# Weight sums of the seven products: from GpSimd to VectorE, with a new order of all steps

## Chip, cores, metric

One Trainium2 chip; the kernel runs on one core. The metric is the device time of one execution in microseconds (us), as the median of several runs, lower is better. PE is TensorE (PEld its weight loads), DVE is VectorE, ACT is ScalarE, POOL is GpSimd, SP is SyncE, which issues most DMAs.

## What is computed

A retention layer with a decaying state is followed by a mixture layer. Batch 4, 8 heads of 64, sequence 768; the second layer is 512 wide with 1024 hidden units. Cut to what matters:

```python
for b in range(nb):                     # blocks of 64 positions
    intra = einsum(einsum(qb, kb) * Dmask, vb)
    out[:, :, sl] = intra + einsum(qb * lam_pow, kv_state)
    kv_state = lam ** 64 * kv_state + einsum(kb * rev_pow, vb)
x = out in (batch, position, 512)
xk = mu_k * x + (1 - mu_k) * x_prev     # x_prev: one position earlier
xr = mu_r * x + (1 - mu_r) * x_prev
k = maximum(xk @ w_k, 0)
v = k * k @ w_v
return sigmoid(xr @ w_r) * v
```

## The kernel before

The 768 positions are six tiles (n = 0 to 5) of 128 positions for all four batches; the 512 channels are four pairs of heads (hp). Products of the second layer are made in float32 quality from two float32r parts of each operand, a high and a low one (`PASSES`, line 423): three matmuls in place of one. ACT makes the high part by a cast (x_high, k_high, piece_high), DVE the low part by a subtraction (x_low, k_low, piece_low).

Tiles 0 and 1 go through the second layer tile by tile. Tiles 2 and 3, and then 4 and 5, go as a pair by a scheme of seven products in place of eight (`strassen`, step M): the weight matrix is cut in quarters 11, 12, 21, 22, and four sums of quarters ("1" to "4") stand beside the quarters as stationary operands; sums of the moving quarters (T1 to T4, sum_moving, step Ts) stand on the other side. KSEQ and VSEQ (line 573) list the seven products of the w_k and of the w_v layer with their operands.

The sums of weights are made once, in the middle of the kernel:

- For w_k: nine additions or subtractions over "lines" of 128 x 1024 (add_lines, step Wp, line 558), in two scratch tiles at home kf0 and kf1, then for each of the four sums a cast to the high part on ACT (sum_high, Wq) and a subtraction for the low part (sum_low, Wr, line 566), in the homes wk0 to wk3, and a store to DRAM (store_sum, Wt). M.0,k,2 to M.0,k,5 read them from SBUF: M.0,k,2 needs Wr of "2", M.0,k,3 that of "1", M.0,k,4 that of "4", M.0,k,5 that of "3".
- For w_v: the quarters are stored to DRAM (keep_set, Ws) and come back in four chunks (load_chunk, Wl, two DMAs of 512 KB each, line 519) into the homes big1, big2, big3 and big1 again (`ROOM`, line 765), which hold the squared hidden units of tile 1 until its V product has read them. For each chunk the high and low parts are joined (join_chunk, Wa, 128 x 1024), four sums of quarters are made (sum_chunk, Wc, 128 x 256 each, one after the other), ACT casts the high part (chunk_high, Wh), the low part is a subtraction (chunk_low, Wd), and two stores go to DRAM (store_chunk, Wo).

Wa, Wc, Wd, Wp and Wr, 37 instructions in all, are issued on POOL. POOL's other work is small: for each mix, copies of 128 x 4 elements that shift the row of positions by one (mix_begin, step i; mix_edge, step z). mix (step f) on DVE waits for them and for ACT's scaled copy (mix_prev, e).

The order of all work is written out by hand as a list of 1222 steps, `ORDER` (line 769). A step is a letter for a function and its arguments; the table is at line 737. Every instruction is kept in program order on its engine (`InOrder`, line 25), SP's DMAs among them, so an engine that waits at a step holds up all its later steps. In the list: A scores, a decay, q decay_queries, U sums, u odd_state, n next_state, B values (0 the first part, 1 the part with the state) for tile and pair; Y a piece of tile 1's V product (six matmuls), o v_out; X a column of the gate product of a late tile, Xo its sigmoid; M.pair,layer,product,column,half six matmuls of a product; j what follows a k product; Th and Td the parts of a moving operand; v, vg, vO the end of a v product, its gate and its store.

```python
    def join_chunk(c):
        t = chunks[c]
        gpsimd.tensor_tensor(t[:, 0], t[:, 0], t[:, 1], op=ALU.add)
```

The functions in full, with the profile's line numbers:

Of the kernel before, what the change touches and what calls it, by code (L numbers as in the profile page):

```python
# [904 lines left out]
```

## Time and profile before

| | us |
|---|---|
| median of 3 runs | 407.19 (406.86 to 409.12) |
| the profiled execution | 404.04 |
| its span, first to last instruction | 402.3 |
| PE busy | 377.5 (94%) |
| DVE busy | 271.7 (68%) |
| ACT busy | 243.5 (61%) |
| POOL busy | 111.2 (28%) |
| mean granted TensorE clock | 0.989 of full |

The profile is of one execution. Busy time is the time in which an engine has an instruction under way, including time in which that instruction is held up after it began. Matmul ends are modelled, so a busy PE is not a PE at its peak. "Idle before, releaser" is what ended an engine's wait.

### The profile page before, as it was taken

Reading aid. Unit: us, or ns where it says so; the run is one execution under the profiler, and the core shown is the slowest. Engines: PE = TensorE matmul, PEld = TensorE weight load, DVE = VectorE, ACT = ScalarE, POOL = GpSimd, SP = SyncE. Lnnn points to the kernel's source line nnn. Section 1 sums busy time; section 2 is a strip of 40 time slices with the busy share of each in tenths; the row PEclk is TensorE's granted clock in tenths of the full one; section 3 lists DMA queues with packets and bytes.
Section 4 is the critical chain, followed back from the end, with each engine's and each line's share of the span. In section 5 each row is a group of like instructions: output and inputs, shape, how many; then the busy total and the mean of one; then the engine's idle time right before and its main releaser. Section 6 shows DMA issues by size and latency. Waiting matters only on the chain.

```text
span 402.3 us, 9529 instructions
## 1 busy us (share of the span) xinstructions
PE 377.5 (94%) x4052; PEld 305.4 (76%) x4052; DVE 271.7 (68%) x349; ACT 243.5 (61%) x385; POOL 111.2 (28%) x191
## 2 busy tenths in 40 slices
...
GB/s 297 408 343 338 350 15 327 163 113 348 318 396 3 105 347 295 339 255 310 184 111 210 287 255 270 220 328 158 58 329 117 104 210 235 124 139 132 194 145 156
DMA packets 29994, 90.89 MB, mean 226 GB/s; under 512 B 2432, under 2 KB 14848, under 8 KB 26240
## 3 DMA queue, kind: packets, MB, share of 16 engines
...
q14 instruction: 10, 0.08, 0.1%
...
## 4 chain that ended last, share of the span: by engine, by line
PE 65%; DVE 12%; ACT 8%; DMA 5%; POOL 5%; issue 2%; SPq 1%; ACTq 0%; POOLq 0%; DVEq 0%
PE dense_m L33 58%; DMA chunk<-sets_v 4%; PE xp_sc L33 4%; POOL chunk L33 3%; DVE t L33 2%; ACT top L33 2%; PE sc_sc L33 2%; DVE qv L33 2%; ACT kf L33 2%; DMA in<-parts 2%; PE u_u L33 1%; DVE xq L33 1%; POOL ts L33 1%; SPq L33 1%; DVE raw L33 1%
## 5 line engine op out<-in xcount | busy, mean ns | idle before, releaser
L33 PE MATMUL dense_m<-t,ws 128*128 128x512 f32 x528 | 122.5, 391 | 0.6 <-DVE snap L33 0.6
L33 PEld LDWEIGHTS dense_m<-t,ws 128*128 128x128 f32 x528 | 98.4, 188 | 21.9 <-DVE snap L33 1.1
L33 PE MATMUL dense_m<-xr,wr 128*128 128x512 f32 x192 | 45.6, 393 | 1.8 <-DVE xr L33 1.8
L33 PE MATMUL dense_m<-xk,wk 128*128 128x512 f32 x192 | 46.7, 397 | 0.0
L33 PE MATMUL dense_m<-wv,k 128*128 128x512 f32 x192 | 45.6, 394 | 0.0
L33 PEld LDWEIGHTS dense_m<-xr,wr 128*128 128x128 f32 x192 | 35.6, 188 | 10.0 <-DVE xr L33 2.6
L33 PEld LDWEIGHTS dense_m<-xk,wk 128*128 128x128 f32 x192 | 35.4, 188 | 8.6 <-issue 0.7
L33 PEld LDWEIGHTS dense_m<-wv,k 128*128 128x128 f32 x192 | 35.5, 188 | 7.8 <-DVE wv L33 0.2
L33 POOL COPY ts<-lastw 128x4 f32<-128x4 f32 x48 | 15.2, 331 | 87.5 <-DVE xr L33 76.2
L33 ACT ACTIVATE c<-c 128x1024 f32<-128x1024 f32 x28 | 29.0, 1058 | 13.9 <-DVE c L33 13.8
L33 ACT ACTIVATE ts<-xp_sc,omu 128x512 f32<-128x512 f32 x40 | 25.9, 688 | 18.9 <-PE xp_sc L33 13.1
L33 POOL TENSOR_TENSOR chunk<-chunk 128x256 f32<-128x256 f32 (+2 forms) x24 | 32.9, 1372 | 7.5 <-DMA chunk<-sets_v 7.0
L33 POOL COPY ts<-ts 128x4 f32<-128x4 f32 x48 | 13.7, 291 | 71.5 <-ACT ts L33 71.4
L33 DVE TENSOR_TENSOR t<-c,t 128x1024 fp32r<-128x1024 f32 x20 | 24.2, 1221 | 10.0 <-ACT t L33 10.0
L33 DVE SCALAR_TENSOR_TENSOR ts<-xp_sc,smalls,ts 128x512 f32<-128x512 f32 x24 | 17.3, 746 | 19.8 <-POOL ts L33 19.2
L33 ACT CAST t<-c 128x1024 fp32r<-128x1024 f32 x20 | 20.9, 1051 | 14.7 <-PE dense_m L33 11.3
L33 ACT COPY mid<-mid 64x256 f32<-64x256 f32 x20 | 7.9, 404 | 29.2 <-DVE mid L33 29.0
L33 DVE TENSOR_TENSOR c<-dense_m,c 128x512 f32<-128x512 f32 x28 | 18.7, 686 | 9.9 <-PE dense_m L33 9.9
L33 DVE TENSOR_TENSOR xr<-ts,xr 128x512 fp32r<-128x512 f32 x24 | 23.1, 966 | 0.9 <-ACT xr L33 0.9
L33 PE MATMUL dense_m<-t,sum 128*128 128x512 f32 x96 | 22.5, 393 | 0.0
L33 PE MATMUL dense_m<-wr,xr 128*128 128x512 f32 x96 | 22.1, 389 | 0.0
L33 DVE TENSOR_TENSOR t<-xq,t 128x1024 fp32r<-128x1024 f32 x10 | 16.0, 1611 | 8.4 <-ACT t L33 8.4
...
## 6 DMA issues: line engine op xcount, KB each, us to landing
...
kin<-kk SPq DMA_DIRECT2D x20, 512.0 KB, 6.0
...
sets_v<-wv SPq DMA_DIRECT2D x8, 512.0 KB, 8.4
chunk<-sets_v SPq DMA_DIRECT2D x8, 512.0 KB, 6.1
sums_v<-chunk SPq DMA_DIRECT2D x8, 512.0 KB, 5.8
...
```

What stands on the lines that cost most here:

```text
L33: return lambda *args, **kw: self.tc.keep_in_program_order(op(*args, **kw))
```

## The change

All of the 37 instructions named above are issued on `vector` in place of `gpsimd`. A chunk may have one room or two separate ones, but each entry of ROOM still has one. The list of steps has the same 1222 steps in a new order, from u0.3 in its tenth line on; the first nine lines stay. Cut to the functions and to the part of the list from Y.113 to M.0,k,3,0,0, and the list's end:

```diff
     def load_chunk(c, s):
         if c not in chunks:
-            chunks[c] = home(ROOM[c], "chunk", [128, 2, 4, 256])
-        sync.dma_start(chunks[c][:, s], SETS["v"][:, :, chunk_at(c, s)])
+            room = ROOM[c]
+            if len(room) == 1:
+                t = home(room[0], "chunk", [128, 2, 4, 256])
+                chunks[c] = t[:, 0], t[:, 1]
+            else:
...
+        sync.dma_start(chunks[c][s], SETS["v"][:, :, chunk_at(c, s)])
 
     def join_chunk(c):
-        t = chunks[c]
-        gpsimd.tensor_tensor(t[:, 0], t[:, 0], t[:, 1], op=ALU.add)
+        lo, hi = chunks[c]
+        vector.tensor_tensor(lo, lo, hi, op=ALU.add)
...
-        gpsimd.tensor_tensor(t[:, o], t[:, a], t[:, b], op=op)
+        vector.tensor_tensor(t[:, o], t[:, a], t[:, b], op=op)
...
-        gpsimd.tensor_tensor(t[:, 0].bitcast(F32R), t[:, 0], t[:, 1], op=ALU.subtract)
+        lo, hi = chunks[c]
+        vector.tensor_tensor(lo.bitcast(F32R), lo, hi, op=ALU.subtract)
...
-        gpsimd.tensor_tensor(line_part(o), line_part(a), line_part(b), op=op)
+        vector.tensor_tensor(line_part(o), line_part(a), line_part(b), op=op)
...
-        gpsimd.tensor_tensor(summed[x][:, :, 0], line_part("AB"[x == "1"]), summed[x][:, :, 1].bitcast(F32), op=ALU.subtract)
+        vector.tensor_tensor(summed[x][:, :, 0], line_part("AB"[x == "1"]), summed[x][:, :, 1].bitcast(F32), op=ALU.subtract)
...
-ROOM = {0: 'big1', 1: 'big2', 2: 'big3', 3: 'big1'}
+ROOM = {0: ('big1',), 1: ('big2',), 2: ('big3',), 3: ('big1',)}
...
-f.021 i.022 Wp.4 y.121 Y.113 A.21 Wl.00 Wl.01 i.023 U.21 L.30 Y.122 u.23 q.23 a.23 Y.121 a.22 Ws.k30 u.22 Y.120 y.120 w.22 g.22
-w.23 Y.123 Wa.0 B.210 Wl.11 L.31 Wl.10 B.211 e.022 Y.132 Wc.01 N.33 e.123 e.023 Wc.03 Y.131 o.12 e.122 i.122 Wc.02 g.31 Wq.=3
-Y.130 Wc.04 o.11 z.022 n.22 Wh.0 z.023 f.023 i.123 Y.133 z.123 z.122 g.30 f.122 Wd.0 k.30 f.123 Wl.20 k.31 n.23 f.022 U.30 x.122
-o.13 Th.0,k,=21,0 i.030 Wo.00 Wa.1 A.30 u.30 y.122 w.30 x.123 o.10 L.33 Wl.21 O.13 Th.0,k,=11,0 a.31 a.30 Wc.11 u.31 i.130 Wc.13
-y.123 X.20 w.31 O.12 q.31 Wc.12 B.300 q.33 i.031 i.131 Wc.14 Td.0,k,=21,0 Wo.01 L.32 B.301 N.32 Wr.=3 Wh.1 n.30 X.21 O.10 e.031
-k.33 Wd.1 O.11 e.130 e.131 X.22 e.030 Wa.2 Wo.10 Wl.31 Xo.20 Wl.30 Xo.21 X.23 z.131 f.131 Wc.21 Td.0,k,=11,0 z.030 x.131 Wc.23
-k.32 z.031 f.030 Wc.22 M.0,k,0,0,0 g.32 q.32 z.130 Xo.22 Wc.24 n.31 Wp.5 y.131 Wh.2 U.31 Wo.11 N.40 f.130 Xo.23 M.0,k,0,1,0 u.33
-g.33 f.031 w.33 Wd.2 x.130 Ts.0,k,T1,0 A.31 j.000 M.0,k,0,2,0 a.32 L.41 a.33 Wa.3 y.130 B.310 u.32 Wo.20 w.32 N.41 L.40 B.311
-Wc.31 e.032 M.0,k,0,3,0 i.132 n.33 Wc.33 e.132 e.033 i.032 i.033 z.132 M.0,k,1,0,0 Th.0,k,T1,0 z.033 f.033 Wc.32 j.001 f.132
-Wc.34 k.41 M.0,k,1,1,0 i.133 z.032 e.133 f.032 Wp.6 Wo.21 N.43 Wh.3 Ts.0,k,T2,0 j.002 j.011 Th.0,k,T2,0 M.0,k,1,2,0 z.133
-Td.0,k,T1,0 Wd.3 Wq.=2 n.32 f.133 k.40 j.010 Wr.=2 g.41 U.40 Td.0,k,T2,0 j.003 Wo.30 x.133 A.40 j.012 x.132 q.41 M.0,k,1,3,0
-Wt.=2 Wp.7 a.41 a.40 Th.0,k,=22,0 y.133 B.400 j.013 i.041 i.141 M.0,k,2,0,0 u.41 Wp.8 Jr.0,=11,1 Td.0,k,=22,0 Jr.0,=11,0
-M.0,k,2,1,0 Wo.31 u.40 N.42 Ts.0,k,T3,0 w.41 Wq.=1 M.0,k,2,2,0 q.40 g.40 Wr.=1 y.132 w.40 Wq.=4 B.401 M.0,k,2,3,0 Wr.=4
-Wi.0,k,=22 L.42 L.43 j.020 Wt.=3 N.51 j.021 M.0,k,3,0,0 e.041 i.140 j.022 z.041 M.0,k,3,1,0 e.140 j.030 j.023 M.0,k,3,2,0 e.141
+e.022 Wp.3 i.031 e.122 i.123 z.123 Y.111 z.122 f.122 z.022 f.123 x.122 Y.110 n.22 q.30 Y.113 f.022 n.23 Th.0,k,=21,0 y.122 A.30
+Wl.01 Wl.00 Th.0,k,=11,0 q.33 U.30 Wp.4 x.123 Y.122 y.123 u.30 i.131 a.31 Y.121 Ws.k30 L.33 a.30 u.31 Y.120 Td.0,k,=21,0 w.31
+g.31 w.30 Y.123 Wa.0 Y.132 Wl.11 Wl.10 Wc.01 Y.131 Wc.03 Wc.02 Wc.04 B.300 o.12 Wh.0 Y.130 Wq.=3 Wd.0 B.301 Wo.00 L.32 n.30
+Y.133 n.31 g.33 o.11 e.031 q.32 e.131 X.20 z.031 Wl.20 i.030 o.13 e.030 Wa.1 O.11 e.130 z.030 z.131 i.130 o.10 X.21 Wc.11 O.10
+O.13 Wr.=3 Wo.01 Wl.21 N.40 Wc.13 f.131 k.32 Wc.12 X.22 k.33 Wc.14 f.030 Wh.1 f.031 i.032 z.130 Xo.21 Wd.1 U.31 f.130 Wo.10
+Wl.31 Wl.30 X.23 u.33 Wp.5 x.130 O.12 g.32 Wa.2 Xo.20 M.0,k,0,0,0 Wc.21 u.32 Wc.23 A.31 j.000 Wc.22 Td.0,k,=11,0 Xo.23
+M.0,k,0,1,0 Wo.11 L.40 L.41 Wc.24 a.33 Wh.2 a.32 x.131 Wd.2 B.310 w.32 Xo.22 y.130 w.33 B.311 y.131 i.132 M.0,k,0,2,0
+Ts.0,k,T1,0 i.133 e.133 i.033 j.001 Wp.6 M.0,k,0,3,0 e.033 Wo.20 N.41 e.032 Wa.3 e.132 M.0,k,1,0,0 z.032 z.133 Th.0,k,T1,0 z.033
+z.132 f.132 M.0,k,1,1,0 g.41 f.033 j.002 j.003 Wc.31 M.0,k,1,2,0 f.032 k.40 Wc.33 i.040 x.132 Ts.0,k,T2,0 Wq.=2 Wo.21 f.133
+Wc.32 Wc.34 j.010 Wh.3 A.40 n.32 Wr.=2 g.40 k.41 M.0,k,1,3,0 Wd.3 Th.0,k,T2,0 Th.0,k,=22,0 n.33 j.011 U.40 Wo.30 Wt.=2
+Td.0,k,T2,0 Jr.0,=11,0 x.133 M.0,k,2,0,0 Td.0,k,T1,0 Wp.7 M.0,k,2,1,0 j.012 u.41 M.0,k,2,2,0 u.40 a.40 w.40 Wo.31 j.013 Wp.8
+Jr.0,=11,1 M.0,k,2,3,0 q.41 Wq.=4 a.41 Wq.=1 Td.0,k,=22,0 Wt.=3 L.42 B.400 w.41 q.40 Wr.=1 B.401 j.020 N.50 Ts.0,k,T3,0 j.022
+M.0,k,3,0,0 j.021 j.023 Ts.0,k,T4,0 M.0,k,3,1,0 j.030 Js.0,=11,0 Wr.=4 M.0,k,3,2,0 j.031 M.0,k,3,3,0 Wt.=1 Wi.0,k,=22 j.032 N.42
...
-M.1,v,6,1,0 v.150 vO.140 vg.141 vg.150 M.1,v,6,0,1 vO.141 M.1,v,6,1,1 v.160 vg.151 vO.160 vO.150 vO.151 v.161 vO.161
+vg.151 M.1,v,6,1,1 vg.150 v.160 vO.150 vO.131 vO.130 v.161 vO.160 vO.141 vO.151 vO.161
```

## Rows read from the trace of the kernel before

**Rows 1.** The page: busy time, share of the span and instructions of an engine.
```profile
PE 377.5 (94%) x4052; PEld 305.4 (76%) x4052; DVE 271.7 (68%) x349; ACT 243.5 (61%) x385; POOL 111.2 (28%) x191
```

**Rows 2.** Busy time by stretch; the first line names the columns.
```profile
core 0: us, PE busy (x) PEld busy (x) DVE busy (x) ACT busy (x) POOL busy (x), PEclk, DMA share, GB/s
...
119.00:143.27 24.27, 24.27 (x226) 19.84 (x225) 11.65 (x15) 6.16 (x12) 13.69 (x13) 1.00 0.31 92
143.27:213.00 69.73, 54.71 (x1040) 43.44 (x1040) 51.99 (x57) 41.80 (x69) 64.53 (x68) 0.95 0.75 256
213.00:380.00 167.00, 167.00 (x1376) 137.12 (x1376) 111.23 (x135) 107.07 (x156) 6.25 (x38) 1.00 0.56 202
```

**Rows 3.** Busy time in slices of 4 us, columns as in rows 2.
```profile
178.00:182.00 4.00, 2.07 (x84) 1.53 (x87) 3.11 (x4) 0.45 (x2) 4.00 (x2) 0.96 0.48 172
182.00:186.00 4.00, 4.00 (x66) 3.41 (x59) 0.69 (x2) 1.95 (x4) 3.49 (x11) 0.61 1.00 260
...
194.00:198.00 4.00, 2.80 (x107) 2.79 (x110) 4.00 (x5) 2.06 (x5) 3.92 (x2) 0.67 0.48 166
```

**Rows 4.** Timeline of PE at the bounds of the stretch: start us, us, engine, what.
```profile
135.58 1.16 PE L33 MATMUL sc_sc<-qv,kin 64*64 64x64 f32 x64
...
137.60 5.74 PE L33 MATMUL dense_m<-wv,k 128*128 128x512 f32 x24
...
211.78 3.47 PE L33 MATMUL dense_m<-t,sum 128*128 128x512 f32 x14
```

**Rows 5.** Timeline of all engines from 202.5 to 213.3.
```profile
206.67 1.21 DVE L33 TENSOR_TENSOR xq<-stage,xq 128x1024 f32<-128x1024 f32 x1
...
206.90 5.98 POOL L33 TENSOR_TENSOR sum<-line,sum 128x1024 fp32r<-128x1024 f32 x2 [1.63 <-ACT sum L33]
...
207.80 2.83 DVE L33 TENSOR_TENSOR qv<-qv,Dt 128x512 f32<-128x512 f32 x1
...
210.69 0.13 PEld L33 LDWEIGHTS xp_sc<-qv,st 64*64 64x64 f32 x1 [3.41 <-DVE qv L33]
```

**Rows 6.** DVE by line and shape, 143.27 to 213: busy us, mean ns | idle before.
```profile
L33 DVE TENSOR_TENSOR xr<-ts,xr 128x512 fp32r<-128x512 f32 x6 | 9.1, 1516 | 0.0
L33 DVE TENSOR_TENSOR t<-xq,t 128x1024 fp32r<-128x1024 f32 x4 | 8.8, 2197 | 0.0
L33 DVE TENSOR_TENSOR qv<-qv,Dt 128x512 f32<-128x512 f32 x5 | 7.1, 1429 | 0.0
...
L33 DVE SCALAR_TENSOR_TENSOR ts<-xp_sc,smalls,ts 128x512 f32<-128x512 f32 x6 | 4.4, 744 | 6.8 <-POOL ts L33 6.7
L33 DVE SCALAR_TENSOR_TENSOR st<-mid,LC,u_xp 128x256 f32<-128x256 f32 x6 | 2.8, 472 | 2.3 <-PE xp_sc L33 2.3
...
L33 DVE TENSOR_TENSOR xq<-xq 128x1024 f32<-128x1024 f32 x1 | 2.4, 2371 | 0.0
```

**Rows 7.** DVE by line and shape, whole span.
```profile
L33 DVE TENSOR_TENSOR xk<-ts,xk 128x512 fp32r<-128x512 f32 x8 | 5.5, 683 | 1.3 <-ACT xk L33 1.3
...
L33 DVE TENSOR_TENSOR c<-c,c 128x1024 f32<-128x1024 f32 x4 | 4.8, 1218 | 0.0
...
L33 DVE TENSOR_TENSOR table<-smalls 128x136 f32<-128x136 f32 x1 | 0.3, 301 | 0.1
```

**Rows 8.** POOL by line and shape, 143.27 to 213.
```profile
L33 POOL TENSOR_TENSOR sum<-line,sum 128x1024 fp32r<-128x1024 f32 x4 | 12.7, 3186 | 1.6 <-ACT sum L33 1.6
L33 POOL TENSOR_TENSOR chunk<-chunk 128x256 f32<-128x256 f32 x16 | 12.5, 784 | 0.5
...
L33 POOL TENSOR_TENSOR chunk<-chunk 128x1024 f32<-128x1024 f32 x4 | 9.9, 2484 | 7.0 <-DMA chunk<-sets_v 7.0
L33 POOL TENSOR_TENSOR line<-line,wk 128x1024 f32<-128x1024 f32 x3 | 7.2, 2392 | 0.0
```

**Rows 9.** Waits, 143.27 to 213: waited for, us in total, times, longest.
```profile
DVE ts L33 <- POOL ts L33: 6.7, 1, 6.7
```

**Rows 10.** The page: DMA issues, KB each, median us to landing.
```profile
chunk<-sets_v SPq DMA_DIRECT2D x8, 512.0 KB, 6.1
```

**Rows 11.** Timeline of ACT's queue: the issue of a store.
```profile
111.21 0.34 ACTq L33 DMA_DIRECT2D out<-rt  x1
```

**Rows 12.** Timeline of POOL: a small copy beside DVE, and one alone.
```profile
187.46 0.19 POOL L33 COPY ts<-ts 128x4 f32<-128x4 f32 x1
...
190.06 1.19 POOL L33 COPY ts<-ts 128x4 f32<-128x4 f32 x1
```

More of the change, by code (lines that the diff above doesn't have):

```diff
@@ L520, in load_chunk @@
         if c not in chunks:
-            chunks[c] = home(ROOM[c], "chunk", [128, 2, 4, 256])
-        sync.dma_start(chunks[c][:, s], SETS["v"][:, :, chunk_at(c, s)])
+            room = ROOM[c]
[3 more added lines that the diff above has]
+            else:
+                for i in range(2):
+                    rt.pop(("h", i), None)
+                chunks[c] = [home(x, "chunk", [128, 4, 256]) for x in room]
+        sync.dma_start(chunks[c][s], SETS["v"][:, :, chunk_at(c, s)])
     def join_chunk(c):
-        t = chunks[c]
-        gpsimd.tensor_tensor(t[:, 0], t[:, 0], t[:, 1], op=ALU.add)
+        lo, hi = chunks[c]
+        vector.tensor_tensor(lo, lo, hi, op=ALU.add)
     def sum_chunk(c, x):
         o, a, b, op = {1: (3, 1, 3, ALU.add), 3: (1, 0, 1, ALU.subtract), 2: (0, 3, 0, ALU.subtract), 4: (2, 2, 0, ALU.subtract)}[x]
-        t = chunks[c][:, 0]
-        gpsimd.tensor_tensor(t[:, o], t[:, a], t[:, b], op=op)
+        t = chunks[c][0]
+        vector.tensor_tensor(t[:, o], t[:, a], t[:, b], op=op)
     def chunk_high(c):
-        t = chunks[c]
-        scalar.copy(t[:, 1].bitcast(F32R), t[:, 0])
+        lo, hi = chunks[c]
+        scalar.copy(hi.bitcast(F32R), lo)
     def chunk_low(c):
-        t = chunks[c]
-        gpsimd.tensor_tensor(t[:, 0].bitcast(F32R), t[:, 0], t[:, 1], op=ALU.subtract)
+        lo, hi = chunks[c]
+        vector.tensor_tensor(lo.bitcast(F32R), lo, hi, op=ALU.subtract)
     def store_chunk(c, s):
-        sync.dma_start(SUMS["v"][:, :, chunk_at(c, s)], chunks[c][:, s])
+        sync.dma_start(SUMS["v"][:, :, chunk_at(c, s)], chunks[c][s])
     scratch, summed = {}, {}
@@ new lines @@
+L.43 N.43 e.041 M.0,k,4,0,0 j.033 Th.0,k,T3,0 M.0,k,4,1,0 Th.0,k,T4,0 Td.0,k,T3,0 Js.0,=11,1 M.0,k,4,2,0 j.041 e.040 M.0,k,4,3,0
+j.040 j.042 M.0,k,5,0,0 j.043 Wi.0,v,=11 Wt.=4 M.0,k,5,1,0 j.050 Td.0,k,T4,0 M.0,k,5,2,0 j.051 y.133 M.0,k,5,3,0 M.0,k,6,0,0
+j.053 Th.0,v,=11,1 j.052 Js.0,=12,1 M.0,k,6,1,0 n.40 Ts.0,v,T1,1 M.0,k,6,2,0 y.132 j.060 e.140 M.0,k,6,3,0 i.140 i.041 j.061
+Th.0,v,=11,0 z.140 z.041 X.30 Jr.0,=21,0 Td.0,v,=11,0 Jr.0,=22,1 q.42 e.141 j.062 Jr.0,=22,0 j.063 X.31 f.041 k.43 i.043 z.040
@@ new lines @@
+Js.0,=12,0 i.141 z.141 f.141 Js.0,=22,0 X.32 Wi.0,v,=2 f.040 Wi.0,v,=1 Xo.31 Ts.0,v,T1,0 Js.0,=21,0 n.41 k.42 Ts.0,v,T2,0 X.33
+g.42 Js.0,=22,1 Td.0,v,=11,1 Xo.30 f.140 Jr.0,=21,1 Ts.0,v,T2,1 M.0,v,0,0,0 Js.0,=21,1 Ts.0,v,T3,0 x.141 A.41 Th.0,v,T2,0
+Ts.0,v,T3,1 U.41 Xo.33 a.42 g.43 M.0,v,0,1,0 Td.0,v,T2,0 L.51 L.50 M.0,v,0,0,1 u.42 a.43 y.141 M.0,v,0,1,1 v.000 Ts.0,v,T4,0
+w.42 Xo.32 B.410 q.43 Wi.0,v,=3 v.001 N.51 u.43 M.0,v,1,0,0 w.43 Th.0,v,T2,1 M.0,v,1,1,0 x.140 Td.0,v,T2,1 Th.0,v,T1,0 B.411
@@ new lines @@
+y.140 Th.0,v,T1,1 M.0,v,1,0,1 e.042 Td.0,v,T1,1 e.142 M.0,v,1,1,1 Td.0,v,T1,0 v.010 k.51 n.42 M.0,v,2,0,0 q.50 v.011 Wi.0,v,=22
+Th.0,v,T3,0 M.0,v,2,1,0 e.043 k.50 q.51 z.043 i.042 M.0,v,2,0,1 i.142 f.043 z.042 Th.0,v,T3,1 z.142 i.143 Td.0,v,T3,0 e.143
+M.0,v,2,1,1 g.51 f.142 z.143 v.020 n.43 M.0,v,3,0,0 Th.0,v,T4,0 Wi.0,v,=12 Ts.0,v,T4,1 v.021 M.0,v,3,1,0 Td.0,v,T3,1 x.142
+Td.0,v,T4,0 U.50 Th.0,v,T4,1 M.0,v,3,0,1 f.143 M.0,v,3,1,1 v.030 f.042 M.0,v,4,0,0 v.031 Th.0,v,=21,0 Wi.0,v,=4 Td.0,v,=21,0
@@ new lines @@
+M.0,v,4,1,0 Td.0,v,T4,1 A.50 Th.0,v,=21,1 L.52 N.52 M.0,v,4,0,1 N.53 x.143 Td.0,v,=21,1 L.53 M.0,v,4,1,1 v.040 a.51 M.0,v,5,0,0
+v.041 u.51 vg.041 w.51 M.0,v,5,1,0 Th.0,v,=22,0 vg.040 y.142 vO.041 M.0,v,5,0,1 g.50 a.50 Th.0,v,=22,1 Td.0,v,=22,0 M.0,v,5,1,1
+k.52 M.0,v,6,0,0 v.051 Td.0,v,=22,1 B.500 q.53 M.0,v,6,1,0 y.143 vg.031 i.151 i.050 k.53 i.150 M.0,v,6,0,1 u.50 vg.051 w.50
+Th.1,k,=11,0 U.51 v.060 B.501 e.050 u.52 M.0,v,6,1,1 g.52 e.150 X.40 g.53 v.061 Wi.1,k,=2 Wi.1,k,=12 Wi.1,k,=11 Th.1,k,=21,0
@@ new lines @@
+Td.1,k,T1,0 M.1,k,2,0,0 Wi.1,k,=4 j.112 M.1,k,2,1,0 j.120 j.113 Jr.1,=11,0 Ts.1,k,T3,0 M.1,k,2,2,0 j.121 e.152 M.1,k,2,3,0 j.122
+M.1,k,3,0,0 j.123 Wi.1,k,=3 Th.1,k,=22,0 M.1,k,3,1,0 Td.1,k,=22,0 M.1,k,3,2,0 j.131 e.153 j.130 M.1,k,3,3,0 z.153 i.153 z.152
+vO.061 f.153 j.132 f.152 x.153 M.1,k,4,0,0 Wi.1,k,=22 Th.1,k,T3,0 M.1,k,4,1,0 Td.1,k,T3,0 j.140 j.133 Js.1,=11,0 Ts.1,k,T4,0
+M.1,k,4,2,0 j.141 Th.1,k,T4,0 M.1,k,4,3,0 Jr.1,=11,1 M.1,k,5,0,0 j.142 Th.1,v,=11,0 M.1,k,5,1,0 j.150 vO.030 Js.1,=12,0
@@ new lines @@
+Td.1,k,T4,0 M.1,k,5,2,0 j.143 j.151 Jr.1,=22,0 M.1,k,5,3,0 j.152 Js.1,=12,1 M.1,k,6,0,0 j.153 Wi.1,v,=2 Jr.1,=22,1 M.1,k,6,1,0
+j.160 Js.1,=11,1 Ts.1,v,T1,0 M.1,k,6,2,0 x.152 vO.060 y.153 Js.1,=22,1 y.152 M.1,k,6,3,0 Th.1,v,=11,1 j.162 j.161 Js.1,=22,0
+X.50 Wi.1,v,=1 Td.1,v,=11,1 Wi.1,v,=11 Td.1,v,=11,0 Ts.1,v,T1,1 X.51 Ts.1,v,T2,1 j.163 X.52 Ts.1,v,T2,0 Xo.51 Th.1,v,T2,0
+Jr.1,=21,1 Td.1,v,T2,0 X.53 Jr.1,=21,0 Ts.1,v,T3,0 Xo.50 M.1,v,0,0,0 Xo.53 M.1,v,0,1,0 M.1,v,0,0,1 M.1,v,0,1,1 v.100 Th.1,v,T2,1
```

67 lines of the change are left out of this document (22 added, 45 removed).

## The prediction

> **What bounds the kernel now.** I read the busy shares first: TensorE (PE) is busy 94% of the span, VectorE (DVE) 68% [rows 1]. A span-wide share hides where the rest is, so next came busy time by stretch [rows 2]. From 213 to 380 us PE has no gap: 167.0 of 167.0 us. From 143.27 to 213 us it is busy 54.7 of 69.7, so 15.0 us are idle there, and two slices of this stretch show a granted clock of 0.61 and 0.67 [rows 3], a mix of the 2.4 and the 1.2 GHz level, the first after a slice in which PE was busy 2.07 of 4 us; by these two 4 x 0.39 + 4 x 0.33 = 2.9 us of its busy time are lost. So some 18 us can be won here; elsewhere there is little but the start and the tail.
>
> The stretch is bounded in the code by Y.123, the last of the 24 matmuls that begin at 137.60, and by M.0,k,3,0,0, which follows M.0,k,2,3,0's six matmuls of 211.78 [rows 4]. Inside it GpSimd (POOL) is busy 64.5 us, nearly throughout, DVE 52.0 [rows 2]. The timeline shows how they meet [rows 5]: DVE's 512-element q.40 takes 2.83 us while POOL works through two sums of 5.98 us, ends some 0.7 us after the first of them must have ended (206.90 + 2.99), and PE's weight load waits 3.41 us for it. DVE's slowness there is not its own work.
>
> How much is it? By shape inside the stretch [rows 6] against the same size elsewhere, 683 ns for 512 elements and 1218 for 1024 [rows 7]: six xr, 6 x (1516 - 683) = 5.0 us; five qv, 5 x (1429 - 683) = 3.7; four t, 4 x (2197 - 1218) = 3.9; one xq, 1.2. Together 13.8 us. All have two inputs in SBUF; those that read PSUM are not stretched.
>
> **The change, part by part.** 37 POOL instructions (13 lines' and sums', 24 chunks') go to DVE.
>
> Removed: POOL's 2.4 to 3.2 us and 784 ns instructions [rows 8]. POOL keeps only the small ts and lastw copies. POOL was not on PE's own path, so its time counts only through what it did to DVE: the 13.8 us above, and the 6.7 us for which DVE's ts mix waited behind POOL's queue [rows 9].
>
> Added, within the stretch of the new order: 4 Wa, 4 Wd, 4 Wp and 3 Wr of 1024 elements and 16 Wc of 256; the other 6 fall before or after it, where DVE has room, and I cost them at nothing. The cover is PE's backlog: from 119 to 143 DVE is busy 11.7 us beside PE's 24.3, from 213 on 111.2 beside 167.0 [rows 2]. If it were gone they would cost 6 x 1.14 = 6.8 us. An undisturbed 1024 takes 1.22 us, and the next instruction starts 0.08 us before its recorded end (206.67 to 207.80 is 1.13, for 1.21) [rows 5, 7], so 15 x 1.14 = 17.1 us. For a 256-element sum of two SBUF inputs there is no row: below it lies the 136-element one at 301 ns, above it the 512-element ones at 683 [rows 7]; on the line between, 0.42, less 0.08, 0.34 us. 16 x 0.34 = 5.4 us, with ends of 3.5 and 9.6. Sum added: 22.5 us.
>
> Moved by the new order: 17 DVE steps leave the stretch (four f of 0.66, two n and two u of 0.39, eight of y, a and q at 0.60, one Td of 1.14: the rows' 744, 472, 683 and 1218 ns less 0.08 [rows 6, 7], in all 10.1 us) and so do four PE groups of 64 small matmuls (B.210, B.211, U.30, A.30). A record of 64 takes 1.16 us [rows 4], and the next group starts before its end; I take 1.08, so 4.3 us. They run earlier in the new order, where PE has no gaps, so these 4.3 us are paid there.
>
> DVE's load in the new stretch: 52.0 - 13.8 - 10.1 + 22.5 = **50.6 us**. PE's: 54.7 - 2.9 - 4.3 = **47.5 us**. So DVE becomes the pace of the stretch, by 3.1 us, and its idle time is added on top. The stretch then counts 50.6 + idle, against 69.7 - 4.3 = 65.4 before: a gain of 14.8 less idle.
>
> The idle time: DVE idled 17.7 us of the stretch before [rows 2]. What made it wait 6.7 us there is gone [rows 9], and with 71 steps in place of 57 its queue is rarely empty. What is left are hand-offs. Wa.0 waits for its chunk at the head: between load and use stand six small DVE steps, Td.21 and Wp.4, about 5.5 us, against a landing of 6.1 us in the median and a wait of 7.0 before [rows 8, 10], so about 1 us. The mixes f wait for ScalarE and then for POOL's edge copy, and n.3x for PE's B.301; I take 3 us for all. Ends: 0, and the whole 17.7. I take **4 us**, nearer to nothing, because the new order puts other DVE steps between each load and its use, and each Wh and its Wd.
>
> Queues passed. On DVE each Wa holds up what stands behind it, v_out (o.12, o.10) and next_state, and PE's X.22 and U.40 wait for these. On SP the loads Wl keep their place right behind the Y steps that free their room; Wl.31 and Wl.30 still wait for chunk 0's two stores, and Wa.3 comes X.23, M.0,k,0,0 to 0,3, A.31 and B.310 later, some 10 us of PE. POOL loses all but its copies, so these start at once. Late next is M.0,k,3,0, which needs Wr.=1, one of the last DVE steps of the stretch.
>
> Tail: the new order leaves vO.131, vO.130 and vO.141 to the end, three stores more in ScalarE's queue at 0.34 us each [rows 11], 1.0 us, of which some may pass before the last product is gated: I take 0.7, ends 0 and 1.0. The new branch for two rooms is never taken: every ROOM has one entry. New order before 143 us and from 213 to 380: no cost, since PE had no gap there and DVE, counted the same way, stays under PE in each stage (closest from M.0,k,6 to M.0,v,0, some 15 of 16 us).
>
> The profiled execution is 404.04 us (span 402.3, 1.7 around it); the median of the runs is 407.19. In the profile: 404.04 - 14.8 + 4 + 0.7 = 393.9. On the median: 407.2 - 10.1 = **397.1 us**, or 393.1 + idle.
>
> **The rivals.**
> *PE keeps pace.* If DVE's small sums run at the low end and 5 more steps slip out of the stretch, PE's 47.5 sets it: 407.2 - (65.4 - 47.5) + 0.7 = 390.0. For it: PE had no gap wherever POOL was quiet. Against it: the sum has DVE ahead by 3.1 us, and eight mixes with hand-offs.
>
> *The lock turned round.* POOL's copies still read SBUF, and DVE now runs 31 more two-input instructions in the stretch. A ts copy that takes 0.19 us alone took 1.19 beside a DVE instruction [rows 12]. If each of the eight mixes left in the stretch waits that long, idle is 8 x 1.19 + 1 = 10.5 and the time 403.6, with 405 in reach. Against it: while DVE waits it holds nothing, so the copy should go ahead. The Trainium skill (SBUF — State Buffer, Who interferes with whom) says that whichever of the two starts first keeps the shared ports for the whole instruction and the other blocks fully; by that rule moving work to VectorE turns the blocking round and does not end it, which is this rival, and the row of 1.19 us agrees with it.
>
> *Chunk loads at the head of DVE's queue* (slower). On POOL a wait for a chunk cost PE nothing: 7.0 us for the first [rows 8]. On DVE it stops everything behind. If each of the four Wa leaves half of 7.0 uncovered, idle is 4 + 14 = 18 and the time 411. It decides from 14.1 us of idle on. For it: chunk 3's room waits for two stores. Against it: some 5.5 us or more of other DVE steps stand between load and use for all four, and DMA landed in 6.1.
>
> That the instructions don't change place can't be: every step is kept in program order.
>
> **How the numbers follow.** Forecast (idle 0 to 8, so 393 to 401): 0.60. PE keeps pace: 0.10. The lock turned: 0.20, of which 0.12 still clearly faster and 0.08 within 0.5%. Chunk waits: 0.10. A measurement can tell about 0.5%, 2.0 us, from no change. So faster 0.60 + 0.10 + 0.12 = 0.82, same 0.08, slower 0.10. The range runs from 391.0, between the forecast's best and PE's pace, to 404.5 at the end of the second rival, leaving out part of the first and the last.
>
> **What would show it.** Right: PE's idle from Y.123 to M.0,k,3,0 down to 6 to 9 us, DVE over 90% busy there, its two-input instructions at 683 and 1218 ns again, the 256-element sums near 0.42 us, POOL under 15 us in the stretch. Wrong: DVE waits for chunk loads of several us; waits of DVE for POOL's ts; a 256-element sum over 0.6 us; new PE gaps before 143 or from 213 to 380; or PE stalls whose releaser is ScalarE.

## The result, and the profile after

The changed kernel takes **397.85 us** (median of 4 runs, 396.99 to 398.87); the kernel before took 407.31 beside it (406.86 to 409.12). The ratio is 0.9761, interval 0.9723 to 0.9798: faster, 0.75 us over the forecast.

The page's busy shares, as [rows 1]:

```profile
PE 376.5 (95%) x4052; PEld 304.0 (77%) x4052; DVE 283.9 (72%) x386; ACT 244.8 (62%) x385; POOL 43.6 (11%) x154
```

Busy time by stretch, columns as in [rows 2]. Y.123 now ends at 152.6 and M.0,k,3,0,0 begins at 205.5, so the first row is the new stretch:

```profile
152.60:205.50 52.90, 47.32 (x787) 36.99 (x785) 49.17 (x71) 32.69 (x53) 6.76 (x23) 1.00 0.83 285
205.50:390.00 184.50, 184.22 (x1453) 150.71 (x1448) 127.95 (x156) 112.37 (x160) 7.74 (x39) 1.00 0.53 190
```

70.1 us have become 52.9. VectorE carries 49.2 of them, TensorE 47.3, GpSimd 6.8, and the clock is 1.00. VectorE's instructions by shape in that stretch:

```profile
L33 DVE TENSOR_TENSOR chunk<-chunk 128x256 f32<-128x256 f32 x16 | 6.7, 421 | 0.3
...
L33 DVE TENSOR_TENSOR chunk<-chunk 128x1024 f32<-128x1024 f32 x4 | 4.9, 1222 | 1.4 <-DMA chunk<-sets_v 1.4
...
L33 DVE TENSOR_TENSOR t<-xq,t 128x1024 fp32r<-128x1024 f32 x3 | 3.7, 1220 | 0.0
L33 DVE SCALAR_TENSOR_TENSOR ts<-xp_sc,smalls,ts 128x512 f32<-128x512 f32 x4 | 3.0, 747 | 0.8 <-POOL ts L33 0.8
...
L33 DVE TENSOR_TENSOR xr<-ts,xr 128x512 fp32r<-128x512 f32 x2 | 1.3, 686 | 0.0
```

xr fell from 1516 to 686 ns and t from 2197 to 1220 [rows 6]; the wait for POOL's ts from 6.7 us to 0.8 [rows 9].

Cut at the bounds of the stretch, the profiled executions divide as follows (the second of the changed kernel is `after_again`, below):

| us | before | after | after again |
|---|---|---|---|
| start to Y.123's end | 143.0 | 152.6 | 150.8 |
| to M.0,k,3,0,0 | 70.1 | 52.9 | 55.2 |
| to the end | 189.2 | 190.7 | 190.7 |
| span | 402.3 | 396.2 | 396.6 |

The spans differ by 6 us and the medians by 9.5: the profiled execution of before, 404.04 us, was quick for that kernel (medians 405.7 to 407.3 in five comparisons). Its granted clock was 0.989 over the span; 42 of the 46 executions of that kernel in the comparisons below show 0.973 to 0.987.

### The profile page after: what moved, and what is told of

Its sections match the earlier page's. It is cut to its first block, busy times and chain, and to the rows that moved or that the text cites. A ratio compares the mean times of both kernels' runs of the same rounds, so it can differ in the third digit from the quotient of the medians.

```text
span 396.2 us, 9516 instructions
## 1 busy us (share of the span) xinstructions
PE 376.5 (95%) x4052; PEld 304.0 (77%) x4052; DVE 283.9 (72%) x386; ACT 244.8 (62%) x385; POOL 43.6 (11%) x154
## 4 chain that ended last, share of the span: by engine, by line
PE 78%; DVE 10%; DMA 5%; issue 2%; POOL 1%; ACT 1%; SPq 1%; ACTq 0%; POOLq 0%
PE dense_m L33 69%; PE xp_sc L33 5%; DMA out<-rt 3%; PE sc_sc L33 3%; DMA in<-parts 2%; PE u_u L33 2%; DVE t L33 1%; DVE rt L33 1%; DVE chunk L33 1%; SPq L33 1%; DVE mv L33 1%; DVE qv L33 1%; POOL ts L33 1%; DVE line L33 1%; DVE ts L33 1%
## 5 line engine op out<-in xcount | busy, mean ns | idle before, releaser
L33 PE MATMUL dense_m<-xk,wk 128*128 128x512 f32 x192 | 48.5, 407 | 0.0
L33 PE MATMUL dense_m<-wv,k 128*128 128x512 f32 x192 | 46.4, 395 | 0.4 <-DVE wv L33 0.4
L33 PE MATMUL dense_m<-xr,wr 128*128 128x512 f32 x192 | 44.8, 390 | 0.0
L33 PEld LDWEIGHTS dense_m<-xk,wk 128*128 128x128 f32 x192 | 36.6, 194 | 9.1 <-issue 0.7
L33 POOL COPY ts<-ts 128x4 f32<-128x4 f32 x48 | 12.6, 266 | 116.6 <-ACT ts L33 116.4
L33 ACT ACTIVATE rt<-dense_m 128x512 f32<-128x512 f32 x24 | 13.9, 596 | 17.9 <-PE dense_m L33 13.8
L33 ACT COPY c<-dense_m 128x512 f32<-128x512 f32 x28 | 15.8, 588 | 13.4 <-PE dense_m L33 13.3
L33 PE MATMUL dense_m<-t,sum 128*128 128x512 f32 x96 | 23.3, 396 | 0.6 <-DVE c L33 0.3
L33 DVE TENSOR_TENSOR xr<-ts,xr 128x512 fp32r<-128x512 f32 x24 | 16.2, 687 | 8.3 <-ACT xr L33 8.3
L33 PEld LDWEIGHTS dense_m<-t,sum 128*128 128x128 f32 x96 | 17.7, 188 | 5.4 <-DVE c L33 1.3
```

The lines of the kernel that those rows point to most:

```text
L33: return lambda *args, **kw: self.tc.keep_in_program_order(op(*args, **kw))
```

## The experiments

Each ran beside the kernel before; a ratio is to it.

### The engine and the order, apart: old_dve and new_pool

old_dve keeps the changed functions and takes the old list of steps:

```diff
-u0.3 h.07 R.000 H.07 c.v0 R.010 Pk. C.v0 R.020 c.v3 Pl. i.110 i.011 R.030 u0.2
+u0.3 h.07 R.000 H.07 c.v0 R.010 Pk. C.v0 R.020 c.v3 Pl. i.011 i.110 i.111 i.010
...
```

> The 37 sums on VectorE (DVE), but in the order of before. Mine (the time comes from DVE no longer being held up by GpSimd (POOL), and the order is needed because DVE becomes the pace): DVE's two-input instructions are back at 683 and 1218 ns, but its load in the stretch is 52.0 - 13.8 + 16 x 1.14 + 16 x 0.34 = 61.9 us with chunk waits of up to 7 us at the head of its queue, so about 73 us for a stretch of 69.7: 405 to 412, no gain. Rival (the engine alone brings it): 396 to 400, as with the new order.

new_pool keeps the new list and gives the sums back to GpSimd, here and in the four other functions:

```diff
     def join_chunk(c):
         lo, hi = chunks[c]
-        vector.tensor_tensor(lo, lo, hi, op=ALU.add)
+        gpsimd.tensor_tensor(lo, lo, hi, op=ALU.add)
```

> The new order, but the 37 sums on POOL as before. Mine: POOL's 64 us of work do not fit in the 53 us that the stretch takes in the new order, and DVE's two-input instructions are stretched again (xr near 1.5 us in place of 0.69): slower than the changed kernel by 5 us or more, 403 to 415. Rival (the new order alone brings it): 396 to 400.

Measured: old_dve 401.39 us (ratio 0.9905, 0.9877 to 0.9933), outside both expectations; new_pool 406.7 (1.002, 0.999 to 1.0049), as expected. Their stretches, old_dve first, columns as above:

```profile
146.66:213.76 67.10, 54.55 (x1042) 43.24 (x1041) 60.27 (x89) 41.78 (x70) 12.05 (x38) 0.95 0.76 266
```

```profile
151.92:213.78 61.86, 49.66 (x786) 38.81 (x784) 35.83 (x40) 31.51 (x51) 53.24 (x54) 0.94 0.70 234
```

| us | old order | new order |
|---|---|---|
| sums on GpSimd | 405.92 | 406.70 |
| sums on VectorE | 401.39 | 397.85 |

The last value is from the first comparison (398.04 in a second one, below); the other three were run together. The order alone gives nothing. The engine alone gives 4.5 us, with the order 8.8. In the old order VectorE has 60.3 us to do in a stretch of 67.1; the new order takes 11 us of it out, and that pays only once GpSimd has left. (The profiled execution of old_dve, 404.86 us, was the longest of its ten; most of the difference lies ahead of the stretch, see "No cost before 143 us" below.)

### What GpSimd did to VectorE: pool_reads and pool_writes

```diff
+    def pool_load(n):
+        m = 256 * n
+        for _ in range(n):
+            gpsimd.tensor_tensor(dum[:, 0:m], flat[:, 0:m], flat[:, 0:m], op=ALU.add)
...
     def join_chunk(c):
         lo, hi = chunks[c]
         vector.tensor_tensor(lo, lo, hi, op=ALU.add)
+        pool_load(2)
```

> The changed kernel, and beside each of the 37 sums that VectorE now makes a useless GpSimd addition over as many elements, which reads a constant from SBUF twice, writes into scratch that nobody reads, and waits for nothing (two of 512 elements for a 1024-wide sum, one of 256 for a 256-wide one). It brings back GpSimd's SBUF traffic and its full queue, and nothing else. My theory (what the old kernel paid was GpSimd's reads stretching VectorE's two-input instructions): xr goes from 0.69 us back to about 1.5, t from 1.22 to about 2.2 where GpSimd is busy, the 256-wide sums from 0.42 to 0.6 or more, VectorE carries 12 to 30 us more between Y.123 and M.0,k,3,0,0, and the time is 408 to 423. Rival (only GpSimd's queue mattered, its ts copies coming late): VectorE's instructions keep 0.69, 1.22 and 0.42, only waits for POOL ts appear, and the time is 398 to 402, the same as in pool_writes.

In pool_writes the loop holds memsets instead:

```diff
-        for _ in range(n):
-            gpsimd.tensor_tensor(dum[:, 0:m], flat[:, 0:m], flat[:, 0:m], op=ALU.add)
+        for _ in range((0, 3, 5)[n]):
+            gpsimd.memset(dum[:, 0:m], 0.0)
```

> The same places and about the same GpSimd time as in pool_reads, but as GpSimd memsets of scratch, which read nothing from SBUF (five of 512 elements for a 1024-wide sum, three of 256 for a 256-wide one). My theory: VectorE's instructions stay at 0.69, 1.22 and 0.42 us; only GpSimd's ts copies come later, and the time is 397 to 402. Rival (any GpSimd instruction stretches VectorE's): as pool_reads, 408 or more.

Measured: pool_reads **417.14 us** (1.0278, 1.0238 to 1.0318), pool_writes **408.23** (1.0055, 1.0029 to 1.0082). The dummies take the same time in both, by their rows in the two pages:

```profile
L33 POOL TENSOR_TENSOR dum<-Dt 128x512 f32<-128x512 f32 (+1 forms) x58 | 71.9, 1239 | 3.8
```

```profile
L33 POOL MEMSET dum<- 128x512 f32 (+1 forms) x153 | 70.3, 459 | 8.2
```

VectorE by shape in the stretch, pool_reads and then pool_writes:

```profile
L33 DVE TENSOR_TENSOR chunk<-chunk 128x256 f32<-128x256 f32 x16 | 11.9, 743 | 0.3
...
L33 DVE TENSOR_TENSOR t<-xq,t 128x1024 fp32r<-128x1024 f32 x3 | 5.6, 1856 | 0.0
...
L33 DVE TENSOR_TENSOR xr<-ts,xr 128x512 fp32r<-128x512 f32 x2 | 2.5, 1312 | 0.0
```

```profile
L33 DVE TENSOR_TENSOR chunk<-chunk 128x256 f32<-128x256 f32 x16 | 6.7, 421 | 0.3
...
L33 DVE TENSOR_TENSOR t<-xq,t 128x1024 fp32r<-128x1024 f32 x3 | 3.6, 1217 | 0.0
...
L33 DVE TENSOR_TENSOR xr<-ts,xr 128x512 fp32r<-128x512 f32 x2 | 1.3, 685 | 0.0
```

Reads stretch VectorE's two-input instructions, writes don't: pool_reads came out as my theory had it. The Trainium skill (SBUF — State Buffer, Who interferes with whom) says just this of a VectorE instruction with two SBUF inputs beside a GpSimd one that reads SBUF or only writes it, and these rows agree. But the full queue costs as much: of 19.1 us over the changed kernel in the same comparison (398.04), 10.2 are there in pool_writes already, where I had expected at most 4. Its time lies in the rival's range, but the rival's reason (any GpSimd instruction stretches VectorE's) is ruled out by these rows. The split into 10.2 and 8.9 us is rough: in the stretch VectorE waits 12.9 us for POOL's ts in pool_writes and 6.8 in pool_reads, and the granted clock is 0.92 and 0.89 there, for 1.00 in the changed kernel. The timeline of pool_writes shows how a full queue costs time:

```profile
192.00 4.60 POOL L33 MEMSET dum<- 128x512 f32 x8
...
197.52 0.75 DVE L33 SCALAR_TENSOR_TENSOR ts<-xp_sc,smalls,ts 128x512 f32<-128x512 f32 x1 [8.93 <-POOL ts L33]
...
201.31 0.74 DVE L33 SCALAR_TENSOR_TENSOR ts<-xp_sc,smalls,ts 128x512 f32<-128x512 f32 x1
...
202.15 1.99 PE L33 MATMUL sc_sc<-qv,kin 64*64 64x64 f32 x64 [9.68 <-issue]
```

A 0.19 us copy stands behind memsets, DVE's mix waits 8.93 us for it, and A.40 starts 0.10 us after the last mix has left the PSUM bank that A.40 writes (201.31 + 0.74). The profile calls that wait "issue"; it is a wait for VectorE.

### Which engine sets the pace now: dve_more and pe_more

```diff
     def chunk_low(c):
         lo, hi = chunks[c]
         vector.tensor_tensor(lo.bitcast(F32R), lo, hi, op=ALU.subtract)
+        for _ in range(2):
+            vector.tensor_tensor(dum, flat[:, 0:512], flat[:, 0:512], op=ALU.add)
```

> The changed kernel with eight useless VectorE additions of 512 elements between Y.123 and M.0,k,3,0,0: two behind each of the four chunk_low steps, reading a constant and writing scratch that nobody reads, which wait for nothing. Eight of 0.60 to 0.68 us are 4.8 to 5.5 us more of VectorE there, and nothing else changes. My theory (VectorE sets the pace of the stretch, with 3.7 us idle of which some can be filled): 3 to 5 us slower than the changed kernel, 401 to 403.5. Rival (TensorE's waits come from ScalarE and from single hand-offs, and VectorE has room): at most 1.5 us slower, 397.5 to 399.5.

```diff
     def late_r(n, j):
-        for hp in range(HP):
-            product(late_bank(n, j), w_of("r", hp // 2, hp % 2, slice(j * 128, j * 128 + 128)), x_of(HP + hp), hp == 0, hp == HP - 1)
+        for _ in range(2 if n == 2 and j in (0, 2) else 1):
+            for hp in range(HP):
+                product(late_bank(n, j), w_of("r", hp // 2, hp % 2, slice(j * 128, j * 128 + 128)), x_of(HP + hp), hp == 0, hp == HP - 1)
```

> The changed kernel with two of tile 2's four late r products, X.20 and X.22, made twice into the same bank (24 more matmuls of 512 columns in the same stretch, about 0.23 us each, 5.5 us; the second pass starts the sum again, so the values stay). My theory (VectorE sets the pace, and TensorE is idle 5.6 us in the stretch): about half of it or more disappears in that idle time, 0 to 3 us slower than the changed kernel, 398 to 401. Rival (TensorE sets the pace and its waits are fixed delays): the whole 5.5 us, 402.5 to 404.

Measured: dve_more 399.53 (0.9838, 0.9811 to 0.9865), pe_more 399.36 (0.9828, 0.9799 to 0.9857): 1.7 and 1.5 us over the changed kernel. The stretches, dve_more first:

```profile
149.37:206.88 57.51, 50.85 (x786) 39.79 (x785) 54.06 (x79) 32.60 (x53) 7.92 (x23) 0.91 0.77 262
```

```profile
150.85:208.41 57.56, 52.41 (x811) 41.32 (x809) 49.09 (x71) 32.71 (x53) 7.26 (x23) 1.00 0.77 262
```

Five microseconds more on either engine cost about the same, some third of themselves in the medians (in the profiles the stretch grew by 3.5 us over the mean of 52.9 and 55.2; dve_more's at a granted clock of 0.91). The profiled execution of pe_more, 400.83 us, was the longest of its four. For dve_more my theory was too strong (3 to 5 expected) and the rival about right; pe_more came out within my theory (0 to 3). "VectorE becomes the pace" doesn't hold: the two are even, and each has slack.

### Moving VectorE's steps: relief, relief2_tail, hand_tail

```diff
-O.13 Wr.=3 Wo.01 Wl.21
+Y.123 Wr.=3 Wa.0 Y.132
...
-w.40 Wo.31 j.013 Wp.8 Jr.0,=11,1 M.0,k,2,3,0 q.41 Wq.=4 a.41 Wq.=1 Td.0,k,=22,0
+M.0,k,3,0,0 Td.0,k,=22,0 u.41 u.40 a.40 a.41 w.40 w.41 q.40 q.41 j.021 j.023
```

> The changed kernel with DVE steps moved within its order: the sum 3 (Wr.=3) runs in the 1.4 us in which DVE waits for the first chunk, n.32 and n.33 come before Wr.=2, and Td.22 and tile 4's u, a, q with B.400 and B.401 come after M.0,k,3,0. In all some 6 of DVE's 49 us leave the way to M.0,k,3,0, and 2 us of PE's. Mine (DVE is the pace of the stretch): PE's idle time of 5.6 us there falls to 2 to 3, time 394.5 to 396. Rival (PE's gaps there come from its own issue or from ScalarE): within 0.8 us of 397.9.

```diff
-Wr.=1 Wt.=3 L.42 j.020 j.022 M.0,k,3,0,0 Td.0,k,=22,0 u.41 u.40
+Wt.=3 L.42 j.020 j.021 j.022 Td.0,k,=22,0 M.0,k,3,0,0 u.41 u.40 j.023 Wq.=1 Wq.=4 Wr.=1
```

> The version meant to beat both: the seven last stores as in tail, VectorE's sum 3 made in the chunk wait and tile 4's first steps behind M.0,k,3,0,0 as in relief, but with ScalarE's copies j.020 to j.023 now ahead of w.40, w.41 and the copies for sums 1 and 4, on which TensorE waited 4.5 us in relief. My theory (TensorE waits in the stretch only for what VectorE or ScalarE finishes late): 1.5 to 3 us under tail, 391.5 to 393, with the stretch near 50 and no wait for ScalarE's c over 0.5 us. Rival (what is moved out comes back behind M.0,k,3,0,0, as in relief): 394 to 395, as tail.

Measured: relief 397.57 (0.9811, 0.9757 to 0.9864), a miss and as its rival; relief2_tail 394.97 (0.9725, 0.9695 to 0.9755), as its rival too. relief2_tail leaves sum 1 out in one place and so doesn't compute the layer: the first of the four groups of M.0,k,3 multiplies by the stored weights, as many matmuls of the same size, which don't wait for sum 1. Even so it missed. In relief the stretch fell to 50.7 us, but what follows it grew from 190.7 to 195.3. PE's timeline in relief:

```profile
193.81 2.57 PE L33 MATMUL dense_m<-t,sum 128*128 128x512 f32 x10 [1.50 <-DVE t L33]
...
200.92 1.65 PE L33 MATMUL dense_m<-t,sum 128*128 128x512 f32 x6 [1.60 <-ACT c L33]
```

Behind M.0,k,3,0,0 the waits became ScalarE's, since its queue holds w.40, which waits for u.40, ahead of the products' copies. hand_tail, tried on mid_tail (below), adds and removes nothing:

```diff
-Ts.0,k,T2,0 Wq.=2 Wo.21 f.133 Wc.32 Wc.34 j.010 Wh.3 A.40 n.32 Wr.=2
+f.133 Ts.0,k,T2,0 Wq.=2 Wo.21 Wc.32 Wc.34 j.010 Th.0,k,T2,0 Wh.3 A.40 n.32 n.33 Wr.=2
...
-U.40 Wo.30 Wt.=2 Td.0,k,T2,0
+U.40 Wt.=2 Td.0,k,T2,0 Wd.3 Wo.30
```

> mid_tail with three of VectorE's steps in another order before M.0,k,2,0,0: f.133, whose result frees the bank that A.40 waits for (1.04 us of TensorE in mid_tail), ahead of the 1.22 us sum for T2; n.33, whose state U.40 waits for (1.39 us), ahead of sum 2's low part; and chunk 3's low part, which no product needs, behind T2's; with it T2's cast ahead of chunk 3's on ScalarE. No work is added or taken away. My theory (after pe_more and dve_more: what is left of TensorE's idle time in the stretch is single hand-offs from VectorE's queue, and a shorter way to each is worth most of its wait): both waits under 0.4 us, M.0,k,3,0,0 1 to 2.4 us earlier against Y.123 than in mid_tail (52.8), and 390.5 to 392 in time. Rival (VectorE's load alone sets the start of M.0,k,3,0,0): the waits move to the products of sum 2 or T1, and the time is mid_tail's 392.7 within 0.7.

Measured: 392.95 us (0.9661, 0.9609 to 0.9712), as the rival has it. PE's timeline, mid_tail and then hand_tail:

```profile
187.03 1.16 PE L33 MATMUL sc_sc<-qv,kin 64*64 64x64 f32 x64 [1.04 <-issue]
...
191.42 0.27 PE L33 MATMUL u_xp<-qv,kin 64*64 64x64 f32 x1 [1.39 <-DVE st L33]
```

```profile
187.02 1.16 PE L33 MATMUL sc_sc<-qv,kin 64*64 64x64 f32 x64
...
197.14 1.66 PE L33 MATMUL dense_m<-t,sum 128*128 128x512 f32 x6 [1.22 <-DVE c L33]
```

The first wait is gone and the second down to 0.24 us; 1.22 us for c and 0.54 for t stand in their place, and the stretch is 54.0 us for 52.8. Shortening these hand-offs moved the waits and gained nothing. That VectorE's load sets the start of M.0,k,3,0,0 is the rival's reading, and not shown by this alone: in this execution (394.03 us, the longest of its four) TensorE had idled 1.1 us more than in mid_tail's before the moved steps, 0.49 for a sigmoid and 1.83 for 1.24 at 179.

### The gap at 103 us: after_again

The changed kernel's trace has a hole inside a group of 64 small products, at 102.9 to 105.1, with every compute engine idle, and a lower clock behind it. Timeline, then two slices:

```profile
102.91 0.22 PE L33 MATMUL xp_sc<-qv,st 64*64 64x64 f32 x1
...
105.11 0.27 PE L33 MATMUL xp_sc<-qv,st 64*64 64x64 f32 x1 [1.99 <-issue]
```

```profile
106.00:108.00 2.00, 2.00 (x6) 1.54 (x6) 0.85 (x2) 1.68 (x4) 0.03 (x1) 0.56 0.97 186
108.00:110.00 2.00, 2.00 (x7) 1.55 (x6) 1.97 (x3) 1.95 (x3) 1.48 (x4) 0.59 0.77 249
```

That is 2.0 us, and 2 x 0.44 + 2 x 0.41 = 1.7 by the clock. No edit in this run:

> The changed kernel once more, for a second profile. My theory: the 2 us in which TensorE issues nothing at 103 us, inside a group of small products, and the low clock behind it belong to that one execution and not to the new order, so they are gone or sit elsewhere here, and the stretch from Y.123 to M.0,k,3,0,0 is again 52.9 us within 1.5; the time is 397.9 within 1. Rival (the new order of the steps makes the gap): a gap of 1.5 to 2.5 us at 102 to 106 again.

Measured: 398.04 us (0.9799, 0.9768 to 0.983). TensorE is busy all of 98 to 114, so the new order doesn't always make the gap; of the twelve traces of the new order and its variants one other, pool_writes, has it (1.70 us at 105). Both traces of the old order are without it, too few to say whether the order makes it likelier. The stretch, 55.2 us, missed my 52.9 by more than 1.5: TensorE waited 1.51 us for mid there, and 0.93 for a sigmoid of rt.

### The tail and ScalarE's queue: tail and mid_tail

```diff
-M.1,v,6,0,1 v.150 vg.151 M.1,v,6,1,1 vg.150 v.160 vO.150 vO.131 vO.130 v.161 vO.160 vO.141 vO.151 vO.161
+M.1,v,6,0,1 vO.130 vO.131 v.150 vg.151 M.1,v,6,1,1 vO.141 vO.151 vg.150 v.160 v.161 vO.150 vO.160 vO.161
```

> The changed kernel with only the stores at its end moved: vO.130, vO.131 and vO.141 are issued as soon as their tiles are ready, ahead of vO.150. In the changed kernel all seven last stores are issued from 389.2 on and the end comes 6.2 us after the last product, against 4.35 before. Mine (the end waits for seven transfers in a row): 1.2 to 2 us less, 395.9 to 396.7. Rival (the last store's own way, issue to landing, sets the end): within 0.4 us of 397.9. The first part is unchanged, so it also shows whether PE's gap of 2.0 us at 103 comes again in another execution.

Measured: **394.4 us** (0.9721, 0.9677 to 0.9764), more than expected. The end of the timeline, changed kernel and then tail (the last rows of VectorE and of ScalarE's queue):

```profile
389.07 1.39 DVE L33 TENSOR_TENSOR rt<-dense_m,rt 128x512 f32<-128x512 f32 x2
389.19 3.80 ACTq L33 DMA_DIRECT2D out_t<-rt  x7
```

```profile
384.99 4.04 ACTq L33 DMA_DIRECT2D out_t<-rt  x6
...
387.28 1.38 DVE L33 TENSOR_TENSOR rt<-dense_m,rt 128x512 f32<-128x512 f32 x2
```

In the changed kernel vO.150 stands ahead of three stores whose data are ready, and all seven go out after 389.19. In tail most are out when VectorE ends.

```diff
-A.31 j.000 Wc.22 Td.0,k,=11,0 Xo.23 M.0,k,0,1,0 Wo.11 L.40 L.41 Wc.24 a.33 Wh.2 a.32 x.131 Wd.2 B.310 w.32 Xo.22 y.130 w.33 B.311
+A.31 j.000 w.32 w.33 Wc.22 Td.0,k,=11,0 x.131 M.0,k,0,1,0 Wo.11 L.40 L.41 Wc.24 a.33 Wh.2 a.32 Wd.2 B.310 Xo.22 Xo.23 y.130 B.311
```

> The version meant to beat both, in another way than relief: the last stores as in tail, and on ScalarE's queue the copies w.32 and w.33 and the cast x.131, whose inputs are ready, moved ahead of the sigmoids Xo.23 and Xo.22 and of the cast of chunk 2's sum, because in tail Xo.23 stands 1.94 us for an earlier store of rt and everything behind it is late: TensorE waits 0.73 us for mid (1.51 in after_again), VectorE 1.14 us for the chunk. My theory (that one wait at the head of ScalarE's queue is passed on to both): no wait of TensorE for mid there, the stretch 1 to 2.5 us shorter than tail's 54.0, and the time 391.5 to 393.5. Rival (the products behind it wait for the sigmoids' banks instead): 394 to 395.5.

Measured: **392.73 us** (0.9672, 0.9637 to 0.9708), the lowest here and as expected, though its interval and tail's overlap. tail's timeline had these two waits:

```profile
174.15 0.60 ACT L33 ACTIVATE rt<-dense_m 128x512 f32<-128x512 f32 x1 [1.94 <-DMA out<-rt]
...
176.83 0.28 PE L33 MATMUL xp_sc<-qv,mid 64*64 64x64 f32 x3 [0.73 <-ACT mid L33]
```

The second is gone in mid_tail, whose stretch is 52.8 us against tail's 54.0.

## Why the prediction was right, step by step

**What is removed** held. The 13.8 us came off whole: the stretched shapes are back at 686 to 688 and 1219 to 1220 ns, and the granted clock in the stretch at 1.00. That GpSimd's reads, and not its load as such, stretched VectorE is shown by pool_reads against pool_writes.

**What is added** held. The 256-wide sum was estimated at 0.42 us and takes 421 ns. VectorE's load was put at 50.6 us in 71 steps and is 49.2 in 71; 0.8 us of the difference are two more stretched shapes of the view of rows 6, at 1741 and 1492 ns, that the removal left out. TensorE's was put at 47.5 and is 47.3 and 47.5.

**Idle time**: 4 us were taken; 3.7 and, in the second profile, 5.9 (55.15 - 49.25) were there. Of the signs, VectorE was 93% and 89% busy (over 90% forecast), TensorE idle 5.6 and 7.7 us (6 to 9 forecast). The step behind this, that VectorE's load plus its idle time gives the stretch, fitted its length, but as a mechanism it was too simple: by dve_more and pe_more neither engine alone sets the pace.

**What is moved** was mis-sized. Four groups at 1.08, 4.3 us, should be paid before Y.123. Up to A.10, the first scores of tile 1, TensorE's steps are the same in both lists. From A.10 to Y.123 the kernel before, after_again and old_dve read:

```profile
54.65:143.04 88.39, 87.79 (x1209) 72.29 (x1208) 52.30 (x75) 43.09 (x78) 18.28 (x39) 1.00 0.62 210
```

```profile
56.87:150.77 93.90, 92.85 (x1465) 76.20 (x1465) 64.37 (x95) 52.26 (x94) 9.00 (x48) 1.00 0.67 228
```

```profile
58.29:146.66 88.37, 87.78 (x1209) 72.30 (x1208) 55.97 (x81) 43.17 (x78) 8.28 (x35) 1.00 0.61 211
```

The 256 matmuls more cost TensorE 5.1 us, 1.27 a group. Part is the return to large matmuls: six right behind a small group take 1.66 us, where 36 in a row take 8.46, that is 1.41 for six:

```profile
147.15 8.46 PE L33 MATMUL dense_m<-wv,k 128*128 128x512 f32 x36
...
156.63 1.66 PE L33 MATMUL dense_m<-wv,k 128*128 128x512 f32 x6
```

**"No cost before 143 us"** was off by less than it looks. The prefix grew by 9.6 and 7.7 us, for 4.3 forecast. The order's part is 93.9 - 88.4 = 5.5 us: these 5.1 and 0.4 more of waits, of which one of 0.65 us for ScalarE at 59 is the longest. The rest comes and goes with the execution. In the changed kernel's profile it is the gap and its clock (97.8 us from A.10 to Y.123, 3.9 more than in after_again). In after_again's it is the start: A.10 begins at 54.65 in the kernel before, at 54.81 and 56.87 in the two profiles of the changed one, and at 58.29 in old_dve, whose list is the old one; the granted clock from 10 to 30 us was 1.00, 1.00, 0.91 and 0.83.

**The tail** was mis-sized: 0.7 us taken, 1.5 measured (190.7 for 189.2), and 2.7 come back when the stores go out early (188.0 in tail). I priced three issues at 0.34 us and not the in-order wait of ready stores behind vO.150.

**The sum**, against the profiled execution: the stretch with its moved work gave 16.1 (mean of 17.2 and 15.0) for 15.1 forecast, the prefix cost 8.7 for 4.3, the tail 1.5 for 0.7; together 6 us for 10.1. With the order's part of the prefix alone, 5.5, it is 9.1. The medians gained 9.5 here and 7.7 beside after_again; the profiled execution I summed against lay 3 us under its median, at a higher granted clock than most. The forecast's mechanism and its largest terms hold; that its total came within 1 us owes something to errors that cancel: the stretch gave 1.0 us more than forecast, the prefix and the tail cost 1.2 and 0.8 more.

**The rivals.** *The lock turned round* exists and costs little: POOL's 0.19 us copies took up to 1.20 us beside VectorE, three in a row 2.77, in the changed kernel's timeline:

```profile
161.86 1.03 POOL L33 COPY ts<-ts 128x4 f32<-128x4 f32 x1 [0.47 <-ACT ts L33]
...
180.04 2.77 POOL L33 COPY ts<-lastw 128x4 f32<-128x4 f32 x3 [12.12 <-ACT mid L33]
```

but VectorE waited only 0.8 us for one, in both profiles. *Chunk loads*: 1.4 us in all, 2.8 in the second profile, not 14. *PE keeps pace*: half true, as pe_more says: a third of added TensorE work shows in the time.
